# Chunk 0's diagonal score blocks: a copy and a VectorE transpose where a round trip through DRAM stood

## Chip, core and metric

One core of a Trainium2 chip runs the whole kernel. The metric is the device time in microseconds (us) of one execution, lower is better. All arrays are float32. The kernel of before takes 641.42 us, the median of three runs that lie between 640.13 and 642.46 us.

## The reference

A delta-rule attention feeds a two-layer network. Cut to what matters here (B = 4, H = 8, S = 768, D = 48; the network has 384 inputs and 2048 hidden units):

```python
k_n = k / (norm(k, axis=-1) + 1e-06)
state = zeros((B, H, D, D))
for t in range(S):
    y[:, :, t] = einsum('bhd,bhde->bhe', q[:, :, t], state)
    v_old = einsum('bhde,bhd->bhe', state, k_n[:, :, t])
    state = state + beta[:, :, t] * einsum('bhd,bhe->bhde', k_n[:, :, t], v[:, :, t] - v_old)
x = y.transpose(0, 2, 1, 3).reshape(B * S, H * D)
h = x @ w_in
out = (h / (1 + exp(-h))) @ w_out
```

The loop over 768 tokens isn't run token by token. It is cut into six chunks of 128 tokens. Inside a chunk the effect of the tokens on one another is a unit triangular system per head, whose matrix comes from the scores k times k, scaled by a step size beta / |k|^2 (with a minus sign). The inverse of that system is made from 32 x 32 diagonal blocks, and in chunk 0 these again from 16 x 16 ones.

## The kernel before

**Tiles and stages.** A chunk's keys lie in one tile with the tokens on the 128 partitions, the 32 heads (4 batches times 8) along the row. TensorE turns them (`turn`), and multiplies keys with keys (`score` with j = 0) into tiles `ap`, one for two batches (g = 0 or 1); the scores of keys with queries (j = 1) follow. `ap` holds for each head the scores of 64 by 64 tokens, of which the 32 x 32 blocks on the diagonal are wanted first. The four row groups of 32 partitions are numbered j = 0 to 3.

**The way of the diagonal blocks in chunk 0.** `block_out` (lines 569 to 578) writes the blocks from `ap` to a DRAM tile `blocks`, four transfers for each g; in chunk 0 the odd j are issued from ScalarE's queue, the even ones from SyncE's. `block_in` (line 580) reads the DRAM tile back in one transfer of 512 KB into `sums_of_w` at AT_G, now with one head on each partition and its 32 x 32 block along the row. The tile x beside it (AT_X) is cleared by GpSimd and gets ones on its diagonal (lines 564, 565).

**The step sizes.** `square` (GpSimd) and `add_squares` (VectorE) sum the squares of the keys. `norm_steps` (line 395) makes from them, on VectorE, an inverse root by three Newton rounds, the norm n, its reciprocal, and the product with beta. For chunk 0 nothing else stands on VectorE between these. Four instructions at line 423 spread the step sizes by row group, six copies (lines 430, 433) lay n out as `n_slot`; a matmul (`block_steps`, line 442) turns the spread sizes, and ScalarE copies them to `step`.

**The inversion.** `invert_first` (line 663) scales the blocks by the step sizes (line 668), then runs 15 rounds of a product (line 676) and a sum (line 680) on VectorE over two 16 x 16 corners of each block at once, multiplies x by the step sizes (line 683), and transposes x in blocks of 32 x 32, once straight and once turned (lines 690, 694), so that heads and tokens change places again. `joins` then builds the 32 x 32 and 64 x 64 inverses with many small matmuls (`corner`, `turned`, `straight`, `merge_half`), whose results ScalarE and VectorE copy out of PSUM.

**The rest.** `inner`, `update`, `old` and `new` run the chunk's recurrence, `hidden` and `combine` the network; after the prologue TensorE does little else than these. The weights arrive as float32 and are narrowed in pieces by ScalarE, VectorE and GpSimd (`narrow`, lines 233 to 246).

**What sets the order.** Each engine runs its instructions in the order in which the code issues them: `pin` chains them. All loads but a few stand in one line on SyncE's queue (`in_line`); a load given to `paced` also waits for the last TensorE instruction issued before it. Later loads hang on a count of TensorE instructions (`loads`, line 1345). `busy` puts matmuls on TensorE whose results nobody reads. The tile `stage` is free until chunk 1's turned keys are put there.

**Names at the change.** The prologue of chunk 0 is the code from line 1289 to 1380: `first_score` and `block_out`, the loads of the second half of the queries, `add_squares`, `beta_of`, `turn` of the queries, `block_in`, `norm_steps(0)`, `first_queries`, `block_steps(0)`, the clearing of `xis` (line 1332), the loads of w_in, k, and v, and the loop over `invert_first`.

Of the kernel before, what the change touches and what calls it, by code (L numbers as in the profile page):

```python
# [10 lines left out]
FP32 = mybir.dt.float32  # L11
U32 = mybir.dt.uint32
ACTF = mybir.ActivationFunctionType
ALU = mybir.AluOpType
# [5 lines left out]
def kernel(  # L20
# [166 lines left out]
    def load_q(c, bs=ALL):  # L187
        if c < NCH:
            load_pair(queries[c], q, c, bs)
# [197 lines left out]
    def add_squares(c, b):  # L387

        pin(nc.vector.tensor_reduce(
            out=sums[c][:, b * H : (b + 1) * H], in_=squared[c, b], axis=AX.X, op=ALU.add  # L390
        ))

    sizes = {}

    def norm_steps(c):

        seed, t, r = (small.tile([P, BH], kind, name=name, bufs=1)[:] for name, kind in (
            ("seed", U32), ("nt", FP32), ("nr", FP32)
        ))
        ss = sums.pop(c)  # L400
        n = small.tile([P, BH], FP32, name="n", bufs=1)
        by_slot = small.tile([P, 2, B * NP], FP32, name="n_slot", bufs=1)
        yield pin(nc.vector.tensor_scalar(
            out=seed, in0=ss.bitcast(U32), scalar1=-0.5, scalar2=1597463007.0,
            op0=ALU.mult, op1=ALU.add,
        ))
# [12 lines left out]
        yield pin(nc.vector.reciprocal(out=r, in_=n[:]))  # L419
        yield pin(nc.vector.tensor_tensor(out=t, in0=r, in1=beta_tok[:, c, :], op=ALU.mult))  # L420
        for j in range(NB):
            rows = slice(T * j, T * (j + 1))
            yield pin(nc.vector.scalar_tensor_tensor(
                out=spread[rows, place(c, j), :], in0=r[rows], scalar=-1.0, in1=t[rows],
                op0=ALU.mult, op1=ALU.mult,
            ))
        of = n[:].rearrange("p (n e) -> p e n", e=2)
        for g, rows in enumerate(HALVES):
            ns = slice(HB * NP * g, HB * NP * (g + 1))
            yield pin(nc.vector.tensor_copy(out=by_slot[rows, :, ns], in_=of[rows, :, ns]))  # L430
            for hf in range(2):
                rest = HALVES[1 - g]
                yield pin(nc.vector.tensor_copy(out=by_slot[rest, hf, ns], in_=of[rest, 1 - hf, ns]))
        sizes[c] = by_slot

    def place(c, j):
# [117 lines left out]
    def block_room(c):  # L554

        if c == 0:
            g, x = (sum_room[:, at : at + T * T] for at in (AT_G, AT_X))
        else:
            g = work.tile([P, T * T], FP32, name="g", tag="g", bufs=1)[:]
            x = (  # L560
                sum_room[:, AT_LAST : AT_LAST + T * T] if c == 1
                else work.tile([P, T * T], FP32, name="x", tag="x", bufs=1)[:]
            )
        pin(nc.gpsimd.memset(x, 0.0))
        pin(nc.gpsimd.memset(x[:, 0 : T * T : T + 1], 1.0))
        g, x = (t.rearrange("p (s t) -> p s t", t=T) for t in (g, x))
        blocks[c] = (tc.dram_tile([P, T, T], FP32, name=f"blocks{c}"), g, x)

    def block_out(c, g):

        there, ap = blocks[c][0], aps[c, g][0]
        for j in range(NB):
            rows, cols = slice(T * j, T * (j + 1)), slice(T * (j % 2), T * (j % 2 + 1))
            at = T * place(c, j) + HH * g
            issue(
                there[at : at + HH].rearrange("n s t -> s n t"),
                ap[rows].rearrange("s u h t -> s (u h) t")[:, :, cols], c == 0 and j % 2 == 1,
            )

    def block_in(c):  # L580
        there, g, _ = blocks[c]
        in_line(nc.sync.dma_start(out=g, in_=there[:]))
# [80 lines left out]
    def invert_first(step):  # L663
# [2 lines left out]
        g2, x2 = corners(AT_G), corners(AT_X)  # L666
        of = step[:].rearrange("p (i m) -> p i m", i=2)
        yield pin(nc.vector.tensor_tensor(
            out=g2, in0=g2, in1=of.unsqueeze(2).to_broadcast([P, 2, Q, Q]), op=ALU.mult
        ))  # L670
        for m in range(Q - 1, 0, -1):
            n = Q - m
# [10 lines left out]
        yield pin(nc.vector.tensor_tensor(  # L683
            out=x2, in0=x2, in1=of.unsqueeze(3).to_broadcast([P, 2, Q, Q]), op=ALU.mult
        ))
# [603 lines left out]
    def first_score(b):  # L1289

        def evacuate(j, e, to, of):
            (by_dve if e else by_act)(to, of)

        score(0, b, (0,), (A, CC), evacuate)
        if b % HB == 1:
            block_out(0, b // HB)

    busy(3)
    for b in range(B):
        square(0, b)  # L1300
    block_room(0)
    for b in range(2):
        turn(0, b, 0, M, b % 2 == 0)
    first_score(0)
    for b in range(2, B):
        turn(0, b, 0, M, b % 2 == 0)
    for b in range(1, B):
        first_score(b)
        add_squares(0, b - 1)
    load_q(0, slice(HB, B))  # L1310
    add_squares(0, B - 1)
    beta_of(0)

    def first_queries(b):
# [3 lines left out]

        score(0, b, (1,), (A, CC), evacuate)

    for b in range(2):
        turn(0, b, 1, M, b == 0)
    block_in(0)
    busy(1)
    for _ in norm_steps(0):
        pass
    first_queries(0)
    busy(3)
    first_queries(1)
# [12 lines left out]
    for b in range(2, B):  # L1342
# [22 lines left out]
            out=to, in0=to, in1=above[:].unsqueeze(1).to_broadcast([P, H, W]), op=ALU.mult  # L1365
        ))

    for n in range(1 + Q):
        done = next(inv)
        if n in (0, 1, 2, 4, 8):  # L1370
            busy(1, done, Sync)
        if n == 10:
            turn(1, 0, 0, M)
        if n == 12:
            turn(1, 1, 0, M)
        if n == 14:
            turn(1, 2, 0, M)
        if n == 15:
            busy(1, done, Sync)
            turn(1, 3, 0, M)  # L1380
# [258 lines left out]
```

## Time and profile before

| what | value |
|---|---|
| median of the runs | 641.42 us (640.13, 641.42, 642.46) |
| span of the profiled execution, first to last instruction | 636.1 us |
| median less that span | 5.3 us |
| TensorE busy | 622.4 us, 98% |
| VectorE, ScalarE, GpSimd busy | 397.5, 214.3, 89.9 us |
| granted TensorE clock, mean | 0.986 |

The whole time of the profiled execution is not listed beside its span, so the 5.3 us stand for what lies around the span. In the rows that follow a row of the timeline or of the chain of waits begins with the start and the duration in us; a row of the groups gives the total busy time and the mean of one in ns; "x2" is a count of merged instructions. In the windows each engine has its busy us and its number of instructions, then come the granted clock as a share of full speed, the DMA share and GB/s.

### The profile page before, as it was taken

The page shows a single profiled execution, that of the slowest core. Times are in us where ns is not written, and L with a number is a line of the kernel's source. Part 1 is how long each engine was busy: PE and PEld are TensorE (multiplying, and loading weights), DVE is VectorE, ACT ScalarE, POOL GpSimd, SP SyncE. Part 2 cuts the span into 40 slices and gives each one's busy share as a digit, 9 for nine tenths or more (in the row PEclk, how much of TensorE's full clock was granted, in tenths as well). Part 3 has the DMA queues.
Part 4 walks back from the last instruction along what each step waited for, and adds up shares of the span by engine and source line. Part 5 has one row for each costly group of instructions (what it writes and reads, how often), then busy time and mean ns, then how long its engine had stood idle before and what let it go on. Part 6 is the DMA issues. An engine that isn't in the chain of part 4 may idle for free.

```text
span 636.1 us, 21387 instructions
## 1 busy us (share of the span) xinstructions
PE 622.4 (98%) x9406; PEld 547.3 (86%) x9406; DVE 397.5 (62%) x910; ACT 214.3 (34%) x500; POOL 89.9 (14%) x92
## 2 busy tenths in 40 slices
PE   7979999999999999999999999999999999999997
PEld 5568788656799989989989989989989989989997
DVE  5786879999677974546974555975455964112112
ACT  3456673423351122451122451122451122441120
POOL 5033721345020020020020010020002000000000
PEclk9779999999999999999999999999999999999999
DMA  7966726350458460459151359232253133010101
GB/s 114 227 159 177 218 67 148 100 99 4 95 105 174 72 104 8 94 107 183 37 91 21 75 124 164 56 84 29 64 117 76 26 75 37 16 38 1 26 0 26
DMA packets 145676, 54.70 MB, mean 86 GB/s; under 512 B 117152, under 2 KB 138912, under 8 KB 145584
## 3 DMA queue, kind: packets, MB, share of 16 engines
q1 hardware_dynamic: 143136, 52.93, 40.5%
q8 instruction: 74, 1.21, 0.8%
q10 hardware_dynamic: 2448, 0.41, 0.4%
q14 instruction: 18, 0.15, 0.1%
HBM read 40.14 MB, written 11.01 MB: 80 GB/s over the span
## 4 chain that ended last, share of the span: by engine, by line
PE 94%; DVE 2%; DMA 1%; issue 1%; ACTq 0%; ACT 0%; POOL 0%; SPq 0%; DVEq 0%; POOLq 0%
PE phid L1046 40%; PE px L1163 17%; PE py L1163 13%; PE po L1090 5%; PE pb_c L840 3%; PE pa L529 2%; PE pb_c L828 2%; PE pyc L919 2%; PE pb_c L1090 2%; PE pb_c L860 2%; PE pyc L906 1%; PE px L782 1%; PE py L782 1%; PE pt L500 1%; DMA sums_of_w<-blocks 1%
## 5 line engine op out<-in xcount | busy, mean ns | idle before, releaser
L1046 PE MATMUL phid<-xT,w_in 128*128 128x256 f32 x1152 | 257.0, 381 | 0.2 <-DVE xT L893 0.2
L1046 PEld LDWEIGHTS phid<-xT,w_in 128*128 128x128 f32 x1152 | 216.4, 190 | 30.2 <-issue 0.9
L1056 ACT ACTIVATE gT<-phid 128x512 f32<-128x512 f32 x88 | 52.5, 597 | 144.8 <-PE phid L1046 140.5
L1144 DVE TENSOR_TENSOR sums_of_g<-gT 128x384 f32<-128x384 f32 (+1 forms) x60 | 30.4, 529 | 65.7 <-ACT gT L1056 55.4
L627 DVE SCALAR_TENSOR_TENSOR rank<-g,step,x 128x31 f32<-128x31 f32 (+15 forms) x124 | 49.8, 401 | 21.7 <-DMA g<-blocks 18.1
L1163 PE MATMUL px<-sums_of_w,sums_of_g 128*128 128x192 f32 x320 | 56.6, 329 | 0.0
L1163 PE MATMUL py<-w_out,sums_of_g 128*128 128x192 f32 x320 | 56.2, 328 | 0.0
L1163 PEld LDWEIGHTS py<-w_out,sums_of_g 128*128 128x128 f32 x320 | 52.3, 190 | 0.3
L1163 PEld LDWEIGHTS px<-sums_of_w,sums_of_g 128*128 128x128 f32 x320 | 52.2, 190 | 0.4
L632 DVE TENSOR_TENSOR x<-x,rank 128x31 f32<-128x31 f32 (+15 forms) x124 | 42.5, 342 | 4.3
L467 POOL TENSOR_TENSOR vf<-vf,n_slot 128x768 f32<-128x768 f32 x10 | 14.8, 1494 | 174.4 <-DMA vf<-in_v_dram 150.4
L544 ACT COPY xT<-pyc 48x128 f32<-48x128 f32 (+2 forms) x126 | 32.7, 260 | 1.7
L488 DVE STREAM_TRANSPOSE kq<-stage 128x512 f32<-128x512 f32 x28 | 28.4, 1115 | 5.2 <-DMA stage<-in_q_dram 5.2
L1163 PE MATMUL py<-w_out,gT 128*128 128x192 f32 x160 | 28.9, 330 | 0.0
L1174 DVE TENSOR_TENSOR o<-o,kept 128x192 f32<-128x192 f32 (+1 forms) x29 | 11.5, 422 | 26.7 <-ACT kept L1171 26.7
L1163 PE MATMUL px<-w_out,gT 128*128 128x192 f32 x160 | 27.9, 327 | 0.0
L1163 PE MATMUL px<-sums_of_w,gT 128*128 128x192 f32 x160 | 27.8, 327 | 0.0
L1163 PEld LDWEIGHTS px<-w_out,gT 128*128 128x128 f32 x160 | 26.5, 190 | 0.6
L550 POOL COPY g<-x 64x256 f32<-64x256 f32 x4 | 5.0, 1242 | 151.9 <-DVE x L635 151.9
L1163 PEld LDWEIGHTS py<-w_out,gT 128*128 128x128 f32 x160 | 26.1, 190 | 0.4
L865 DVE TENSOR_TENSOR state<-state,pb_c 128x384 f32<-128x384 f32 x22 | 11.2, 550 | 24.1 <-PE pb_c L860 24.1
L1163 PEld LDWEIGHTS px<-sums_of_w,gT 128*128 128x128 f32 x160 | 26.2, 190 | 0.1
(222 smaller groups left out, 931.2 us busy)
## 6 DMA issues: line engine op xcount, KB each, us to landing
vf<-in_v_dram SPq DMA_DIRECT2D x48, 96.0 KB, 2.8
out_dram<-o SPq DMA_DIRECT2D x42, 96.0 KB, 2.2
w_out<-in_moe_w_in_dram SPq DMA_DIRECT2D x4, 768.0 KB, 4.7
sums_of_w<-in_moe_w_out_dram SPq DMA_DIRECT2D x4, 768.0 KB, 4.1
blocks<-ap SPq DMA_DIRECT2D x44, 64.0 KB, 1.9
g<-blocks SPq DMA_DIRECT2D x5, 512.0 KB, 3.5
kb<-in_k_dram SPq DMA_DIRECT2D x12, 192.0 KB, 4.2
kb<-in_k_dram SPq DMA_DIRECT2D x24, 96.0 KB, 4.3
```

Source lines behind the costliest of these rows:

```text
L467: pin(nc.gpsimd.tensor_tensor(out=vf, in0=vf, in1=of, op=ALU.mult))
L488: pin(nc.vector.transpose(out=kqs[c, b][:, :, j, :].rearrange("p a (i m) -> p a m i", i=T), in_=src.rearrange("p a (m d) -> p a m d", d=D) ...
L529: pin(nc.tensor.matmul(pa[e][half, p * n * W : (p + 1) * n * W], lhsT=kq[rows, p, 0, half], rhs=kq[rows, p, js[0] : js[-1] + 1, half], sta ...
L544: return pin(nc.scalar.copy(to, of))
L627: pin(nc.vector.scalar_tensor_tensor(out=tv, in0=g[:, 0:m, m : m + 1].to_broadcast([P, m, n]), scalar=step[:, m : m + 1], in1=x[:, m : m + ...
L632: yield pin(nc.vector.tensor_tensor(out=x[:, 0:m, m:T], in0=x[:, 0:m, m:T], in1=tv, op=ALU.add))
L840: yield pin(nc.tensor.matmul(pz[rows, n * D : (n + 1) * D], lhsT=xis[g][rows, u * H + 2 * p + e, :], rhs=vfs[c][rows, hf, g * HB + u, p, : ...
L1046: pin(nc.tensor.matmul(ph[:, j * GT : (j + 1) * GT], lhsT=w_in[:, a, (2 * f + j) * P : (2 * f + j + 1) * P], rhs=xTs[c, hf][:, a, :], star ...
L1056: pin(nc.scalar.activation(out=hidden_of(c, hf, f), in_=ph[:], func=ACTF.Silu, scale=-0.5 if in_blocks(c) else 0.5))
L1090: pin(nc.tensor.matmul(pos[i][:, 0:DM], lhsT=hidden_of(0, hf, f // 2)[:, at : at + C], rhs=w_outs[f // HFF][:, f % HFF, :], start=(f == 0) ...
L1144: pin(nc.vector.tensor_tensor(out=sums_of_g[:, k, fs], in0=of[0], in1=of[1], op=op))
L1163: pin(nc.tensor.matmul(to, lhsT=at, rhs=quarter(f, *b) if isinstance(b, tuple) else sums_of_w[b][:, f], start=start and f == 0, stop=f == ...
```

## The change

Chunk 0 no longer sends its diagonal blocks through DRAM. A view `diagonal` of the tile `stage` takes them: eight copies of 32 partitions by 512 elements, from `ap` (32 of each 64 columns) to a dense row, six on GpSimd (all four of g = 0, the first two of g = 1) and two on ScalarE. One VectorE transpose in 32 x 32 blocks then puts heads on the partitions and writes the place from which `invert_first` reads. The step sizes of chunk 0 are made by one VectorE instruction on all partitions and turned by one VectorE transpose into `step`; the four spreading instructions, the matmul and ScalarE's copy are gone for chunk 0, and the six copies to `n_slot` go to GpSimd.

GpSimd writes the step sizes on x's diagonal instead of ones, so that the last multiplication of x by them falls away. In exchange, the blocks are scaled along their other index (`unsqueeze(3)` for `unsqueeze(2)` at line 668).

The order moves too. The second half of the queries is loaded at the start of the prologue; the loads of w_in 0, keys 1, w_in 1 and v 0 are issued ahead of the queries' turning, w_in 0 without `paced`. The four `add_squares` stand between the turns and scores. ScalarE takes both of the first two turns of queries out of PSUM. One `busy` matmul is added before the last two turns.

```diff
-        for j in range(NB):
+        if c == 0:
+            size = small.tile([P, T], FP32, name="step")
+            pin(nc.vector.scalar_tensor_tensor(
+                out=t, in0=r, scalar=-1.0, in1=t, op0=ALU.mult, op1=ALU.mult
+            ))
+            pin(nc.vector.transpose(out=size[:], in_=t))
+            step_of[0] = size
+        for j in range(NB if c > 0 else 0):
...
+        engine = nc.vector if c > 0 else nc.gpsimd
...
-            yield pin(nc.vector.tensor_copy(out=by_slot[rows, :, ns], in_=of[rows, :, ns]))
+            yield pin(engine.tensor_copy(out=by_slot[rows, :, ns], in_=of[rows, :, ns]))
...
-        pin(nc.gpsimd.memset(x[:, 0 : T * T : T + 1], 1.0))
+        if c > 0:
+            pin(nc.gpsimd.memset(x[:, 0 : T * T : T + 1], 1.0))
...
-            out=g2, in0=g2, in1=of.unsqueeze(2).to_broadcast([P, 2, Q, Q]), op=ALU.mult
+            out=g2, in0=g2, in1=of.unsqueeze(3).to_broadcast([P, 2, Q, Q]), op=ALU.mult
...
-        yield pin(nc.vector.tensor_tensor(
-            out=x2, in0=x2, in1=of.unsqueeze(3).to_broadcast([P, 2, Q, Q]), op=ALU.mult
-        ))
...
-        if b % HB == 1:
-            block_out(0, b // HB)
+    diagonal = stage[:, 0 : BH * T].rearrange("p (n t) -> p n t", t=T)
+
+    def diagonal_blocks(g, engines):
+
+        for j, by in enumerate(engines):
+            rows, cols = slice(T * j, T * (j + 1)), slice(T * (j % 2), T * (j % 2 + 1))
+            by(diagonal[rows, HH * g : HH * (g + 1)], aps[0, g][0][rows].rearrange("s u h t -> s (u h) t")[:, :, cols])
+
+    load_q(0, slice(HB, B))
     busy(3)
     for b in range(B):
         square(0, b)
     block_room(0)
+    add_squares(0, 0)
     for b in range(2):
         turn(0, b, 0, M, b % 2 == 0)
+    add_squares(0, 1)
     first_score(0)
     for b in range(2, B):
         turn(0, b, 0, M, b % 2 == 0)
-    for b in range(1, B):
-        first_score(b)
-        add_squares(0, b - 1)
-    load_q(0, slice(HB, B))
+    add_squares(0, 2)
+    first_score(1)
+    diagonal_blocks(0, (by_pool, by_pool, by_pool, by_pool))
+    first_score(2)
+    first_score(3)
+    diagonal_blocks(1, (by_pool, by_pool, by_act, by_act))
     add_squares(0, B - 1)
     beta_of(0)
...
+    fetch_w_in(0)
+    load_k(1)
+    fetch_w_in(1)
+    load_v(0)
     for b in range(2):
-        turn(0, b, 1, M, b == 0)
-    block_in(0)
+        turn(0, b, 1, M)
...
-    step = block_steps(0)
+    step = step_of[0]
+    of_step = blocks[0][2].rearrange("p s t -> p (s t)")[:, 0 : T * T : T + 1]
+    pin(nc.gpsimd.tensor_copy(out=of_step, in_=step[:]))
+    pin(nc.vector.transpose(
+        out=blocks[0][1].rearrange("p s t -> p t s"), in_=diagonal.rearrange("p n t -> p t n")
+    ))
     for t in xis:
         pin(nc.gpsimd.memset(t, 0.0))
-    paced(fetch_w_in, 0)
-    load_k(1)
-    fetch_w_in(1)
-    load_v(0)
     for c in range(1, NCH):
         beta_of(c)
-    busy(1)
+    busy(2)
...
-    for n in range(1 + Q):
+    for n in range(Q):
```

More of the change, by code (lines that the diff above doesn't have):

```diff
@@ L391, in add_squares @@
         ))
-    sizes = {}
+    sizes, step_of = {}, {}
     def norm_steps(c):
@@ L429, in norm_steps @@
             ns = slice(HB * NP * g, HB * NP * (g + 1))
-            yield pin(nc.vector.tensor_copy(out=by_slot[rows, :, ns], in_=of[rows, :, ns]))
+            yield pin(engine.tensor_copy(out=by_slot[rows, :, ns], in_=of[rows, :, ns]))
             for hf in range(2):
                 rest = HALVES[1 - g]
-                yield pin(nc.vector.tensor_copy(out=by_slot[rest, hf, ns], in_=of[rest, 1 - hf, ns]))
+                yield pin(engine.tensor_copy(out=by_slot[rest, hf, ns], in_=of[rest, 1 - hf, ns]))
         sizes[c] = by_slot
@@ L564, in block_room @@
         pin(nc.gpsimd.memset(x, 0.0))
[L565 removed]
+        if c > 0:
+            pin(nc.gpsimd.memset(x[:, 0 : T * T : T + 1], 1.0))
         g, x = (t.rearrange("p (s t) -> p s t", t=T) for t in (g, x))
[L567 removed]
+        blocks[c] = (tc.dram_tile([P, T, T], FP32, name=f"blocks{c}") if c > 0 else None, g, x)
     def block_out(c, g):
@@ L576, in block_out @@
                 there[at : at + HH].rearrange("n s t -> s n t"),
-                ap[rows].rearrange("s u h t -> s (u h) t")[:, :, cols], c == 0 and j % 2 == 1,
+                ap[rows].rearrange("s u h t -> s (u h) t")[:, :, cols],
             )
```

## The prediction

> **What bounds the kernel now.** I read the page first, for the share of each engine over the whole and the chain that ended last.
>
> ```profile
> span 636.1 us, 21387 instructions
> PE 622.4 (98%) x9406; PEld 547.3 (86%) x9406; DVE 397.5 (62%) x910; ACT 214.3 (34%) x500; POOL 89.9 (14%) x92
> PE 94%; DVE 2%; DMA 1%; issue 1%; ACTq 0%; ACT 0%; POOL 0%; SPq 0%; DVEq 0%; POOLq 0%
> ```
>
> TensorE is the bound, and the change takes no work from it but one matmul. So it can only pay where the chain leaves TensorE: the 2% of VectorE and 1% of DMA. The chain of waits of the first 95 us shows where that is.
>
> ```profile
> 10.68 0.44 DVE ap L547
> 11.18 0.38 ACTq L104
> 14.14 2.76 DMA blocks<-ap
> 17.05 4.91 DMA sums_of_w<-blocks
> 22.06 0.70 DVE sums_of_w L668
> 22.85 0.22 DVE rank L676
> 31.52 0.99 DVE sums_of_w L683
> 32.54 1.04 DVE sums_of_w L690
> 33.58 1.82 DVE sums_of_w L694
> 52.46 1.53 PE phid L1046 x6
> ```
>
> The last row is the first matmul of the hidden layer. From 11.18 us on, the end hangs on the eight transfers out, then on the one back, which lands at 21.96; only then can VectorE scale the blocks (22.06) and begin the rounds (22.85). It ends the last transpose at 35.40. What moves these two ends moves all behind them, as long as nothing else becomes late: from there the chain goes through TensorE to the end, and the later loads hang on TensorE's count, so they move along. So I ask when the rounds begin, and how long they take. For that I read the timeline of VectorE from 10 to 23 us.
>
> ```profile
> 12.27 0.41 DVE L547 COPY ap<-pb_c 128x256 f32<-128x256 f32 x1
> 12.60 1.00 DVE L389 TENSOR_REDUCE ss<-sq 128x8 f32<-128x384 f32 x2
> 13.52 0.68 DVE L506 TENSOR_SCALAR kq<-pt 128x512 f32<-128x512 f32 x1
> 14.11 0.17 DVE L403 TENSOR_SCALAR seed<-ss 128x32 uint32<-128x32 uint32 x1
> 16.80 0.35 DVE L419 RECIPROCAL nr<-n 128x32 f32<-128x32 f32 x1
> 17.26 0.19 DVE L420 TENSOR_TENSOR nt<-nr,beta_tok 128x32 f32<-128x32 f32 x1
> 17.49 0.77 DVE L423 SCALAR_TENSOR_TENSOR spread<-nr,nt 32x32 f32<-32x32 f32 x4
> 22.06 0.69 DVE L668 TENSOR_TENSOR sums_of_w<-sums_of_w,step 128x512 f32<-128x512 f32 x1 [3.01 <-DMA sums_of_w<-blocks]
> ```
>
> The norm takes 14.11 to 17.49: fourteen instructions, 12 of them up to the reciprocal in 2.69 us, 0.224 each. VectorE is free at 19.05 and waits 3.01 us. So the transfers hide the norm now; without them the norm itself is late next.
>
> **The change part by part.** *The way through DRAM* goes: 8 transfers out, one in, and ScalarE's two stops for issuing them. *The end of the scores.* Two of the four reductions (0.5 each by the row with x2) go ahead into gaps in which VectorE waited for TensorE, and the query copy of 0.68 goes to ScalarE. So the copy that starts at 12.27 can start as soon as the last scores are there, and TensorE's row for them is the first here; the second is a ScalarE copy of the size of the new ones:
>
> ```profile
> 11.30 0.22 PE L529 MATMUL pb_c<-kq 48*64 48x64 f32 x1
> 141.88 0.62 ACT L544 COPY xi<-up 32x512 f32<-32x512 f32 x1
> ```
>
> They end at 11.52; the copy ends at 11.95, the last reduction at 12.45, and the norm begins near 12.5 in place of 14.11. ScalarE, freed of issuing, makes its two copies (0.62 each) after its last score copy near 11.95 and reaches beta near 13.2, before VectorE asks for it.
>
> *If nothing disturbed it,* the norm's 3.38 us end at 15.9; the product on all partitions and the small transpose are two more steps of 0.23 (a 128x32 instruction), 16.35; the transpose of the blocks has the shape of line 694, 1.82 on the chain, 18.2; the scaling 0.79 (22.06 to 22.85), 19.0. The rounds begin 3.85 early. At the end the multiplication by the step sizes is gone: 31.52 to 32.54, 1.02. Together 4.87. That is the bound on the good side.
>
> *But six copies now stand on GpSimd beside the norm.* What one costs I take from the groups, and how GpSimd and VectorE get on with each other from their timelines at 128 us, where GpSimd has instructions back to back and VectorE rounds of the same kind as here.
>
> ```profile
> L550 POOL COPY xi<-up 32x512 f32<-32x512 f32 x2 | 1.6, 777 | 8.4 <-DVE up L607 8.4
> L691 POOL COPY sums_of_w<-pick 128x512 f32<-128x512 f32 x1 | 0.6, 632 | 18.3 <-DVE rank L676 18.3
> L550 POOL COPY g<-x 64x256 f32<-64x256 f32 x4 | 5.0, 1242 | 151.9 <-DVE x L635 151.9
> L334 POOL COPY pick<-ident 32x32 f32<-32x32 f32 x4 | 0.8, 203 | 0.2
> 127.98 1.88 POOL L246 TENSOR_TENSOR w_out<-w_out,sums_of_w 128x768 int32<-128x768 int32 x1 [1.62 <-ACT sums_of_w L234]
> 129.82 3.09 POOL L467 TENSOR_TENSOR vf<-vf,n_slot 128x768 f32<-128x768 f32 x2
> 276.33 2.91 POOL L467 TENSOR_TENSOR vf<-vf,n_slot 128x768 f32<-128x768 f32 x2 [45.43 <-DMA vf<-in_v_dram]
> 128.20 1.86 DVE L632 TENSOR_TENSOR sums_of_w<-sums_of_w,rank 128x175 f32<-128x175 f32 x1
> 130.09 1.48 DVE L627 SCALAR_TENSOR_TENSOR rank<-g,step,sums_of_w 128x156 f32<-128x156 f32 x1
> 131.61 1.48 DVE L632 TENSOR_TENSOR sums_of_w<-sums_of_w,rank 128x156 f32<-128x156 f32 x1
> 133.12 0.36 DVE L627 SCALAR_TENSOR_TENSOR rank<-g,step,sums_of_w 128x135 f32<-128x135 f32 x1
> ```
>
> Three VectorE instructions that would need under 0.4 us (the row at 133.12 is such a one) end at 130.06, 131.57 and 133.09: each 0.2 or so after a GpSimd instruction ended (129.86, then about 131.2 and 132.91). One VectorE instruction gets through per GpSimd instruction, while GpSimd loses only 0.09 each (3.09 against 2.91 for the pair). The Trainium skill, "SBUF — State Buffer", section "Who interferes with whom", says that a VectorE instruction with two SBUF inputs and a GpSimd one that reads SBUF block each other for the whole instruction; it speaks against this change, and by it the sum is the smaller one below, without it the 4.87. The trace agrees, by the three rows.
>
> Twelve of the norm's instructions, with the new product, have two inputs in SBUF. The copies can begin at 11.15, when the second batch's scores are out (10.68 + 0.44 on the chain) and GpSimd is free of clearing x, as its row shows.
>
> ```profile
> 10.08 0.95 POOL L564 MEMSET sums_of_w<- 128x1024 f32 x1
> ```
>
> A copy has the shape of the 777 ns row, of which some is the same quarrel, since VectorE copied beside it; 632 ns is the bound below, 1242 ns (a column read across the row) the one above. I take a pace of 0.76 per copy, hold-up included, nearest the row of its own shape. Six end at 15.7. In that time the norm passes its seed and one further instruction at the end of each copy from the third to the sixth: four, the last ending at 15.9. Seven remain to n, 7 x 0.224, 17.45; the reciprocal 0.46 (16.80 to 17.26), 17.9. Now the six copies to `n_slot`, which waited for n on GpSimd, run beside it at about 0.2 each (the 203 ns row): the two products wait some 0.12 each, 18.6; the small transpose 18.85; the blocks 20.7; the scaling 21.5. The rounds begin 22.85 - 21.5 = 1.35 early, and with the 1.02 the sum is 2.37, call it 2.4. Bounds by the pace: 0.70 gives 2.7, 1.31 (the 1242 ns row with the hold-up) gives a loss, worked out below.
>
> *Costed at nothing:* the small copy that writes x's diagonal (0.2) and the clearing of `xis` are queued on GpSimd behind `n_slot` and end under the transpose of the blocks (1.82); without that cover the 0.2 would count. Who waits for the diagonal is the first round at 21.5. The scaling along the other index has the same operands and count. The 16 transfers of w_in 0, keys 1, w_in 1 and v 0 that are pulled ahead on SyncE's queue stand in front of nothing that the prologue reads; the second half of the queries comes earlier, and TensorE no longer waits for it as here:
>
> ```profile
> 20.84 0.63 PE L500 MATMUL pt<-ident,z 128*128 128x128 f32 x4 [0.41 <-DMA z<-in_q_dram]
> ```
>
> That wait lies off the chain, so it earns nothing. The extra `busy` matmul is hidden in TensorE's own wait for the first round.
>
> So the span becomes 636.1 - 2.4 = 633.7. The median of the runs stands 5.3 above the span of before; with that unchanged the time is 639.0 us.
>
> **The rivals.** *A: the lock doesn't bite.* If the small products of 0.19 us slip between copies, or the copies are done by the time that they come, the whole 4.87 is had: 636.5 us. For it: the first two copies are over before the norm begins. Against: the rows at 128 us, and no row with two inputs that ran free beside such a GpSimd instruction.
>
> *B: the copies are slow and the norm waits longer than the transfers did.* Place: GpSimd's six copies. At 1.31 each they end at 19.0; the norm has five of its two-input steps by then (19.2), n comes at 20.55, the reciprocal at 21.0, the products 21.7, the turned step size 21.95, the blocks 23.8, the scaling 24.6: 1.75 late, less 1.02, a loss of 0.7, 642.1 us. Between a pace of 0.76 (gain 2.4) and 1.31 (loss 0.7) the point from which the time is lost lies near 1.18. For it: the only other strided copy on GpSimd took 1242 ns. Against: that one reads single columns, while these read runs of 32 elements, as the 777 ns row writes them.
>
> *C: the clock eats it.* TensorE's granted clock falls twice in the start.
>
> ```profile
> 21.00:22.00 1.00, 1.00 (x8) 0.88 (x7) 0.00 (x0) 0.50 (x1) 0.00 (x0) 0.69 0.95 336
> 28.00:29.00 1.00, 1.00 (x4) 0.61 (x3) 0.90 (x4) 0.00 (x0) 0.00 (x0) 0.90 0.91 218
> 38.00:39.00 1.00, 0.09 (x11) 0.00 (x0) 0.97 (x2) 0.73 (x2) 0.37 (x1) 0.72 0.73 215
> 48.00:49.00 1.00, 1.00 (x50) 1.00 (x52) 0.87 (x2) 0.00 (x0) 0.00 (x0) 0.66 0.06 16
> ```
>
> Between 21.4 and 28.2, and between 38.4 and 48.7, it is half: 6.8 and 10.3 us, two and three steps of 3.4. The first fall lies under VectorE's rounds; the second lies on the small matmuls of the chain. Where work moves against these steps, one step more at half clock costs up to 1.7 us, one less gains as much: 640.7 or 637.3. The Trainium skill, "TensorE: Matmul & The Clock Gate", section "What's actually happening", has a free-running window of 3413 ns that decides by the activity in it; the trace agrees with its 6.8 and 10.3 us. Against a loss: TensorE's work moves as a whole, so the step is as likely to help. A loss of one step is what I count as C, 640.7.
>
> **How the numbers follow.** Chances: the forecast 0.50, A 0.20, B 0.13, C 0.17. About 0.3%, 1.9 us, is what a measurement of this kernel can tell from no change; so faster means under 639.5, slower over 643.3. The forecast's own range is 638.2 to 640.0 (paces of 0.70 to 0.90), and I put 0.38 of its 0.50 under 639.5; with A that is 0.58. Slower takes 0.08: the part of B where the clock also loses a step (642.1 + 1.7 = 643.8) and 0.03 for what I have not seen. The rest, 0.34, is within 0.3%. The range reaches from a little below A, 636.0, to B, 642.2.
>
> **What would show it.** In the changed profile I expect: no transfer of blocks before 70 us; six copies of GpSimd from 11.15 to about 15.7 at 0.65 to 0.8 each; instructions of the norm at 0.6 to 0.8 us beside them and 0.19 after; the transpose of the blocks at 18.85, the scaling at 20.7, the first round at 21.5; the rounds themselves unchanged, 8.7 us; the last transpose ending near 33.0 and the same lead kept at the first hidden-layer matmul (52.46 before). Wrong would be: a norm with 0.19 throughout (A); copies over 1.18 us (B); rounds that begin early while the lead is lost between 33 and 52 us (C, or a wait that I have not named). Wrong altogether would be a transpose of the blocks that isn't what VectorE waits for, but ScalarE's two copies or beta.

## The result, and the profile after

| | before | changed |
|---|---|---|
| median of the runs, us | 641.13 (20 runs, 639.34 to 642.46) | 638.86 (20 runs, 636.76 to 640.35) |
| ratio, 95% interval | | 0.9965 (0.9955 to 0.9975) |
| profiled execution: its time, span | not listed, 636.1 | 638.56, 636.8 |

The changed kernel is 2.27 us faster; 639.0 was forecast. Two spans of profiled executions can't show that: 636.1 before stands against 636.8 after. Every later run gives its time beside its span: the difference is 1.8 us here (638.56 - 636.8), 1.7 to 1.9 in all kernels but that of experiment 6, which has 2.1 to 2.2. The 5.3 us that the prediction put "around the span" were therefore mostly something else: the first trace of before shows an execution of about 637.9 us (an estimate, 636.1 + 1.8), quicker than any of the 20 runs in the table. So the kernel before was traced a second time, and the changed kernel too.

> The kernel before, for a second trace. Theory (the first trace of before was a quick execution: its span of 636.1 us lies 3 us under what its median leaves): the head is as in the first trace (first round 22.8, last transpose ends 35.4 us, both within 0.3), and the 3 us show behind it, on the way to the first hidden-layer matmul or after 94 us, where single waits come and go. Rival (before's own head is slower as a rule than its first trace showed): the first round begins after 23.3 us.

> The changed kernel unchanged, beside the next three, for a second trace and a second set of times on the same chip. Theory: the gain over before is 2.3 us, give or take 0.6; the first round begins at 20.8 us, the last transpose ends near 32.3, and TensorE's clock is half for three or four steps of 3.4 us between 33 and 50 us. Rival (the trace of after was an odd one): the first round or the last transpose move by more than 0.3 us.

Run again, the kernel before took 640.86 us against itself at 640.59 (ratio 0.9996, 0.9982 to 1.0011); the changed kernel 637.93 against 640.63 (0.9955, 0.9944 to 0.9967). Their spans, 639.1 and 636.8, now lie as the medians do. In both traces the start differs from the first trace by more than the 0.3 us that the expectations allowed: before begins its rounds at 22.38 where it had 22.85, the changed kernel at 21.29 where it had 20.78. For the changed kernel that is the rival on record. Of its 0.51 us, 0.35 lie ahead of the norm (the first keys land later and the squares start at 6.65, 6.24 in the first trace); the norm itself has the other 0.16.

First the page of the changed kernel: the span, the engines' busy times, the chain's shares by engine.

```profile
span 636.8 us, 21379 instructions
PE 620.8 (97%) x9406; PEld 545.9 (86%) x9406; DVE 398.3 (63%) x901; ACT 216.1 (34%) x502; POOL 94.7 (15%) x104
PE 94%; DVE 3%; issue 1%; DMA 1%; ACT 0%; SPq 0%; POOL 0%; POOLq 0%; DVEq 0%
```

TensorE's 94% is as before; VectorE's share of the chain has grown from 2% to 3%: the norm stands on it now, where the transfers of the blocks stood. The timeline of VectorE in the changed kernel shows that norm and what follows it.

```profile
12.07 0.54 DVE L389 TENSOR_REDUCE ss<-sq 128x8 f32<-128x384 f32 x1
12.65 0.18 DVE L403 TENSOR_SCALAR seed<-ss 128x32 uint32<-128x32 uint32 x1
12.87 0.48 DVE L409 SCALAR_TENSOR_TENSOR nt<-ss,seed 128x32 f32<-128x32 f32 x1
13.39 0.62 DVE L412 TENSOR_TENSOR nt<-nt,seed 128x32 f32<-128x32 f32 x1
14.04 0.62 DVE L413 SCALAR_TENSOR_TENSOR nr<-nt,seed 128x32 f32<-128x32 f32 x1
14.69 0.61 DVE L409 SCALAR_TENSOR_TENSOR nt<-ss,nr 128x32 f32<-128x32 f32 x1
15.34 0.19 DVE L412 TENSOR_TENSOR nt<-nt,nr 128x32 f32<-128x32 f32 x1
...
16.70 0.18 DVE L418 TENSOR_SCALAR n<-nt 128x32 f32<-128x32 f32 x1
...
18.00 1.94 DVE L1353 STREAM_TRANSPOSE sums_of_w<-stage 128x1024 f32<-128x1024 f32 x1
19.98 0.69 DVE L677 TENSOR_TENSOR sums_of_w<-sums_of_w,step 128x512 f32<-128x512 f32 x1
20.78 0.21 DVE L685 TENSOR_TENSOR rank<-sums_of_w 128x30 f32<-128x30 f32 x1
...
30.36 1.95 DVE L700 STREAM_TRANSPOSE sums_of_w<-sums_of_w 128x1024 f32<-128x1024 f32 x1
```

The GpSimd timeline of the changed kernel has the six copies beside it, and ScalarE's has its two.

```profile
11.36 3.90 POOL L558 COPY stage<-ap 32x512 f32<-32x512 f32 x6
...
18.21 0.24 POOL L1352 COPY sums_of_w<-step 128x32 f32<-128x32 f32 x1
```

```profile
12.25 1.24 ACT L552 COPY stage<-ap 32x512 f32<-32x512 f32 x2 [0.19 <-DVE ap L555]
13.52 0.20 ACT L364 ACTIVATE beta_tok<-pb 128x32 f32<-128x32 f32 x1
```

The six copies end at 15.26, 0.65 each. Between 12.87 and 15.30 four instructions of the norm get through, at 0.48 to 0.62 us; those after it take 0.19. The reduction above them has one input and takes 0.54, as without the copies (experiment 3). The seed, with one input too, begins here as the second copy ends (12.66) and takes 0.18. In the second trace of the changed kernel it begins just after that (12.99) and is held up like the others. This is VectorE there, and the copies beside it:

```profile
13.00 0.64 DVE L403 TENSOR_SCALAR seed<-ss 128x32 uint32<-128x32 uint32 x1
13.68 0.62 DVE L409 SCALAR_TENSOR_TENSOR nt<-ss,seed 128x32 f32<-128x32 f32 x1
...
14.98 0.61 DVE L413 SCALAR_TENSOR_TENSOR nr<-nt,seed 128x32 f32<-128x32 f32 x1
```

```profile
11.71 3.84 POOL L558 COPY stage<-ap 32x512 f32<-32x512 f32 x6 [0.75 <-DVE ap L555]
```

Four get through beside the last four copies here as well, but the seed is one of them. It takes 0.64 in experiment 4 too. So two inputs are not the whole condition; experiment 8 comes back to this.

Blocks (15.26) and beta (13.72) are there long before VectorE asks for them, so the norm alone sets when the rounds begin: 20.78. What was 35.40 in the first trace of before, the end of the last transpose, is now 32.31. The chain of waits of the second trace of before shows the same places, with the last row from near 95 us, where the long runs of hidden-layer matmuls begin.

```profile
16.45 5.05 DMA sums_of_w<-blocks
...
22.38 0.21 DVE rank L676
33.10 1.81 DVE sums_of_w L694
53.05 1.53 PE phid L1046 x6
95.58 4.51 PE phid L1046 x20
```

And the chain of the changed kernel at the two later places.

```profile
50.68 1.53 PE phid L1052 x6
93.05 7.10 PE phid L1052 x32
```

The lead over this trace is 22.38 - 20.78 = 1.6 us at the first round, 34.91 - 32.31 = 2.6 at the last transpose, 53.05 - 50.68 = 2.4 at the first hidden matmul, 95.58 - 93.05 = 2.5 near 95 us, and 639.1 - 636.8 = 2.3 at the end. What is won in the first 33 us reaches the end nearly whole. Against the first trace it shrank from 3.1 to 1.8 by the first hidden matmul and was gone at the end; that was that execution's doing. The two traces of before part in the same way: the second is 0.5 us ahead at the last transpose, 0.6 behind at the first hidden matmul, 1.4 behind near 95 us and 3.0 at the end.

The traces of all kernels at these places (us; "way" is the time from the last transpose to the second half of xT, the input of the hidden layer):

| | first round | last transpose ends | way | xT written | span |
|---|---|---|---|---|---|
| before, first trace | 22.85 | 35.40 | 16.9 | 52.32 | 636.1 |
| before again | 22.38 | 34.91 | 18.0 | 52.90 | 639.1 |
| changed | 20.78 | 32.31 | 18.2 | 50.54 | 636.8 |
| changed again | 21.29 | 32.80 | 17.9 | 50.66 | 636.8 |
| final product back | 20.79 | 33.33 | 18.5 | 51.85 | 637.1 |
| product gone alone | 22.39 | 33.89 | 17.6 | 51.48 | 637.2 |
| no GpSimd copies | 19.22 | 30.75 | 18.3 | 49.00 | 633.8 |
| loads late | 20.54 | 32.06 | 18.6 | 50.64 | 638.4 |
| four copies by ScalarE | 20.16 | 31.70 | 17.8 | 49.48 | 635.1 |
| the same, x cleared earlier | 19.55 | 31.07 | 19.4 | 50.47 | 637.9 |
| roots in PSUM | 18.95 | 30.47 | 19.9 | 50.33 | 636.1 |

### The profile page after: what moved, and what is told of

It reads as the page before. It is cut to its first block, busy times and chain, and to the rows that moved or that the text cites. A ratio compares the mean times of both kernels' runs of the same rounds, so it can differ in the third digit from the quotient of the medians.

```text
span 636.8 us, 21379 instructions
## 1 busy us (share of the span) xinstructions
PE 620.8 (97%) x9406; PEld 545.9 (86%) x9406; DVE 398.3 (63%) x901; ACT 216.1 (34%) x502; POOL 94.7 (15%) x104
## 4 chain that ended last, share of the span: by engine, by line
PE 94%; DVE 3%; issue 1%; DMA 1%; ACT 0%; SPq 0%; POOL 0%; POOLq 0%; DVEq 0%
PE phid L1052 40%; PE px L1169 17%; PE py L1169 13%; PE po L1096 5%; PE pb_c L846 3%; PE pa L537 3%; PE pb_c L834 2%; PE pyc L925 2%; PE pb_c L1096 2%; PE pb_c L866 2%; PE pyc L912 1%; PE px L788 1%; PE py L788 1%; PE pb_c L537 1%; PE pt L508 1%
```

## The experiments

**1. The final product back.** The step sizes leave x's diagonal; the multiplication after the rounds stands again.

```diff
-        if c > 0:
-            pin(nc.gpsimd.memset(x[:, 0 : T * T : T + 1], 1.0))
+        pin(nc.gpsimd.memset(x[:, 0 : T * T : T + 1], 1.0))
...
-            out=g2, in0=g2, in1=of.unsqueeze(3).to_broadcast([P, 2, Q, Q]), op=ALU.mult
+            out=g2, in0=g2, in1=of.unsqueeze(2).to_broadcast([P, 2, Q, Q]), op=ALU.mult
...
+        yield pin(nc.vector.tensor_tensor(
+            out=x2, in0=x2, in1=of.unsqueeze(3).to_broadcast([P, 2, Q, Q]), op=ALU.mult
+        ))
...
-    of_step = blocks[0][2].rearrange("p s t -> p (s t)")[:, 0 : T * T : T + 1]
-    pin(nc.gpsimd.tensor_copy(out=of_step, in_=step[:]))
...
```

> The changed kernel with one part undone: ones on x's diagonal, the blocks scaled along the old index, and the last multiplication of x by the step sizes back. Theory (the lead at VectorE's last transpose is 2.07 us from rounds that begin early and 1.02 us from the product that is gone; what is left of it reaches the end one for one): the last transpose ends 1.0 us later than in the changed kernel (near 33.3 us in place of 32.3) and the gain over before falls from 2.3 to about 1.2 us. Rival (the clock's steps decide, a microsecond of lead is not worth a microsecond): the gain stays within 0.4 us of 2.3, or goes altogether.

637.93 us against 639.85 (0.9975, 0.9960 to 0.9989). The chain of waits of this kernel, behind the last sum of the rounds:

```profile
29.45 0.99 DVE sums_of_w L691
30.47 1.04 DVE sums_of_w L698
```

The product costs 30.47 - 29.45 = 1.02 on VectorE, and xT comes 1.2 to 1.3 later than in the changed kernel. In the time the theory isn't borne out: the gain over before is 1.9 us, within the 0.4 of 2.3 that the rival allowed, and not about 1.2. Experiment 4, the changed kernel but for its loads and measured beside the same runs of before, gains 2.25; against that the product costs 0.3 us, and the intervals overlap.

**2. That part alone, on the kernel before.** The step sizes go on x's diagonal, the blocks are scaled along the other index, the product is gone; nothing else of the change.

```diff
-        pin(nc.gpsimd.memset(x[:, 0 : T * T : T + 1], 1.0))
+        if c > 0:
+            pin(nc.gpsimd.memset(x[:, 0 : T * T : T + 1], 1.0))
...
-        yield pin(nc.vector.tensor_tensor(
-            out=x2, in0=x2, in1=of.unsqueeze(3).to_broadcast([P, 2, Q, Q]), op=ALU.mult
-        ))
...
+    of_step = blocks[0][2].rearrange("p s t -> p (s t)")[:, 0 : T * T : T + 1]
+    pin(nc.gpsimd.tensor_copy(out=of_step, in_=step[:]))
```

> The kernel before with one part of the change alone: GpSimd puts the step sizes on x's diagonal, the blocks are scaled along the other index, and the last product is gone; the way through DRAM stays. Theory: the first round stays at 22.85 us (the step sizes are there by 19.0 and the diagonal by 19.3, the transfer lands at 21.96), the last transpose ends 1.02 us earlier (34.4), and the time falls by 1.0 us, give or take 0.6. Rival (the scaling along the other index costs what the product saved, or the diagonal comes late): no change.

640.67 us against 640.59 (0.9995, 0.9982 to 1.0008). The last transpose ends at 33.89, 1.02 before the 34.91 of "before again", and xT comes 1.4 earlier; in the time 1.0 us was expected and none is seen (the interval reaches from 1.2 us faster to 0.5 slower). The 1.02 us are shown at VectorE, twice; that the end gets them is not.

**3. GpSimd's copies taken away.** The copies of ScalarE stay; six of the eight blocks' rows are zeros, written early. This asks what the copies cost the norm.

```diff
-    diagonal_blocks(0, (by_pool, by_pool, by_pool, by_pool))
...
-    diagonal_blocks(1, (by_pool, by_pool, by_act, by_act))
+    diagonal_blocks(1, (None, None, by_act, by_act))
```

> The changed kernel without GpSimd's six copies into the dense tile: that part of it is cleared early instead, so chunk 0's inverse is made from a quarter of the blocks only. Theory of the lock: the four norm steps that took 0.48, 0.62, 0.62 and 0.61 us take 0.19 each, the norm and all behind it come 1.5 us earlier than in the changed kernel (first round near 19.2 us instead of 20.78), and the gain over before is 3.3 to 3.9 us. Rival (they waited for something else, such as ScalarE or the reductions): the four steps stay above 0.4 us and the first round stays near 20.8.

635.92 us against 639.85 (0.9941, 0.9926 to 0.9956). VectorE's timeline of this kernel:

```profile
12.91 0.19 DVE L410 SCALAR_TENSOR_TENSOR nt<-ss,seed 128x32 f32<-128x32 f32 x1
...
13.82 0.19 DVE L413 TENSOR_TENSOR nt<-nt,nr 128x32 f32<-128x32 f32 x1
...
19.22 0.20 DVE L686 TENSOR_TENSOR rank<-sums_of_w 128x30 f32<-128x30 f32 x1
```

The same four instructions go from 12.91 to 13.82, 0.91 us, in place of 12.87 to 15.34, 2.47: the hold-up is 1.56, and the first round comes 1.56 earlier than in the changed kernel. All of it reaches xT (49.00 against 50.54). In the time it is 3.9 us below before, where the changed kernel's two measurements have 2.3 and 2.7.

**4. The loads late.** w_in 0 paced again, and the loads of w_in 0, keys 1, w_in 1 and v 0 back where they were.

```diff
-    fetch_w_in(0)
-    load_k(1)
-    fetch_w_in(1)
-    load_v(0)
     for b in range(2):
...
         pin(nc.gpsimd.memset(t, 0.0))
+    paced(fetch_w_in, 0)
+    load_k(1)
+    fetch_w_in(1)
+    load_v(0)
```

> The changed kernel with the loads of w_in 0, keys 1, w_in 1 and v 0 put back to their old place, w_in 0 again waiting for TensorE. Theory (these loads stand in front of nothing that the path reads): no change against the changed kernel, a gain over before of 2.3 us, give or take 0.5. Rival (part of the gain is that weights and v lie ready earlier): the gain falls under 1.5 us and waits for w_in or vf show between 32 and 60 us.

637.60 us against 639.85 (0.9973, 0.9958 to 0.9988), and first round, last transpose and xT stand as in the changed kernel. The early loads are not where the gain is. Its trace has a span of 638.4 for another reason; the chain of waits shows it.

```profile
91.58 3.52 DMA xT<-part
95.24 5.81 PE phid L1052 x18
```

TensorE stood still from 93.54 to 95.24 for one transfer of xT; the window from 96 to 97 us then has a granted clock of 0.50. The changed kernel's two traces have no such wait there.

**5. Fewer copies on GpSimd.** ScalarE makes all four of the second half.

```diff
-    diagonal_blocks(1, (by_pool, by_pool, by_act, by_act))
+    diagonal_blocks(1, (by_act, by_act, by_act, by_act))
```

> The changed kernel with all four copies of the second half on ScalarE, so that GpSimd makes four. Theory of the lock: only two norm steps are held up instead of four, the first round begins 0.85 us earlier (near 19.9 us) and the gain over before grows to about 3 us, unless ScalarE's copies, now four of 0.62 us from 12.2 on, bring beta later than VectorE asks for it (near 16.5 us). Rival (the transposes wait for the copies, not the norm): the first round does not move, or moves later.

638.65 us against 639.85 (0.9976, 0.9959 to 0.9993): a gain of 1.2 us where about 3 was expected, so not faster than the changed kernel. VectorE's timeline shows the lock where it was foreseen, with two norm steps held up and not four.

```profile
13.08 0.48 DVE L409 SCALAR_TENSOR_TENSOR nt<-ss,seed 128x32 f32<-128x32 f32 x1
13.60 0.62 DVE L412 TENSOR_TENSOR nt<-nt,seed 128x32 f32<-128x32 f32 x1
14.25 0.19 DVE L413 SCALAR_TENSOR_TENSOR nr<-nt,seed 128x32 f32<-128x32 f32 x1
```

The rounds begin at 20.16, 0.62 earlier (0.85 was expected). In this execution the lead also reached xT, written at 49.48, 1.1 earlier than in the changed kernel; 0.6 of it stands at VectorE's first instruction behind the transposes (L730, 31.57 against 32.18), the rest came with a clock that was half for 10.2 us and not 13.7. Why the median shows none of it, this trace doesn't tell; the next experiment has a trace in which the lead is lost.

**6. The same, and x cleared before the squares,** while GpSimd waits for keys, so that its copies can start sooner.

```diff
     busy(3)
+    block_room(0)
     for b in range(B):
         square(0, b)
-    block_room(0)
```

> The changed kernel with four GpSimd copies in place of six (ScalarE makes all of the second half) and x cleared before the squares, while GpSimd waits for the keys, so that the copies begin 0.2 us earlier. Theory of the lock: one or two norm steps are held up, the first round begins at 19.9 us or earlier, 0.9 before the changed kernel, and the gain over before is about 3 us. Rival (what is won at the head is lost behind it, as in the run with four copies): first round as said, and a gain of no more than 2.3 us.

639.22 us against 640.59 (0.9971, 0.9956 to 0.9987). The rounds begin at 19.55 and the last transpose ends at 31.07, 1.2 earlier than in the changed kernel, yet xT is written at 50.47, against 50.54 and 50.66 there. That is the rival: the gain is 1.4 us and not about 3. The chain of waits of this kernel no longer passes through the norm.

```profile
13.78 0.61 ACT stage L552
14.41 0.20 ACT beta_tok L364
14.61 0.50 ACT kq L518
15.85 3.41 PE pb_c L347 x6
31.48 0.13 PE pl L723 x2
32.16 0.08 DVE sums_of_w L730
```

ScalarE's four copies (the last at 13.78) make the query copies behind them late, TensorE's scores wait for those, and TensorE then comes to the corner matmuls (L723) only at 31.41; VectorE waits 1.09 us for them, and its first instruction behind the transposes starts at 32.16, as in the changed kernel (32.18).

The late query copies are not all of it. The six rows of `busy` at 15.85 take 3.41 us here and 2.20 in the changed kernel (at 14.88), and the window on them shows why.

```profile
17.00:18.00 1.00, 1.00 (x3) 0.56 (x2) 1.00 (x1) 0.00 (x0) 1.00 (x2) 0.50 1.08 170
```

The granted clock is half from 16.5 to 20.0. From these `busy` matmuls to the next of beta (L361) TensorE needs 4.36 us (15.78 to 20.14), and 2.76 both in the changed kernel and in experiment 5: the 1.60 between them are more than the 1.09 that VectorE waited. In experiment 5 TensorE waits as long for the query copies, at full clock, and the lead stands. So in this trace the half clock, and not the late query copies alone, takes the lead away. TensorE had stood 2.0 us for the query copies just before, and a third trace with four copies on ScalarE (the second kernel of experiment 7) shows such a fall (17.3 to 20.7) after the same wait, while no trace with six copies on GpSimd has one there. That the wait brings the fall, and that this is what the medians of both experiments show, was not tested.

How much room TensorE had is told by the view of what TensorE waits for between 10 and 51 us, first in the changed kernel, then in this one.

```profile
PE pb_c L347 <- DVE sums_of_w L689: 1.3, 1, 1.3
PE pa L537 <- ACT kq L518: 1.0, 2, 0.8
```

```profile
PE pa L537 <- ACT kq L518: 2.3, 2, 2.0
```

A row gives the total wait, the number of waits and the longest. In the changed kernel TensorE stands 1.3 us at a `busy` matmul that is paced by the rounds: so much later it may come without cost. Here, and in experiment 5, the wait for the query copies has grown by 1.3 and the other row is gone. In experiment 3 that row is gone too, with nothing in its place, and there VectorE's 1.56 us reached xT whole.

**7. Fuller TensorE, against the clock.** The granted clock is half for 13.7 us between 34 and 48 us in the changed kernel. Nine more matmuls whose results nobody reads were spread over that stretch, in the changed kernel, in that of experiment 5, and in the kernel before.

```diff
...
+        if n == 13:
+            busy(1, done, Sync)
...
-        lambda: (),
+        lambda: busy(2, room=M),
...
-        lambda: (fill(1),),
+        lambda: (fill(1), busy(3, room=M),),
...
-        lambda: (fill(1), begin_next(),),
+        lambda: (fill(1), begin_next(), busy(3, room=M),),
```

> The changed kernel with nine more matmuls whose result nobody reads, put where TensorE waits between the last rounds and the merges (one at round 13, two after the corners, three after the straight products, three after the first merges). Theory (the half clock over the merges costs part of the lead): the half clock between 34 and 48 us is shortened or gone, the way from the last transpose to the first hidden-layer matmul falls from 18.4 us to under 17.4, and the time falls by 1 to 2 us against the changed kernel. Rival (the merges wait for VectorE and ScalarE, not for TensorE's clock): the clock rises, the way stays within 0.4 us of 18.4 and the time doesn't change; or the added matmuls get in the way and it grows.

> The same nine matmuls, and ScalarE makes all four copies of the second half as in the run of that change alone, whose first round began 0.6 us early without a gain that could be measured. Theory (the 0.6 us are there, and were lost in the clock's steps): 0.6 us faster than the kernel with the nine matmuls alone. Rival (ScalarE's later copies cost elsewhere): no faster, or slower, with a later evacuation of the first query scores to show for it.

> The kernel before with the same nine matmuls in the same places. With the clock dealt with alike on both sides the difference to the changed kernel with nine matmuls is the lead of the change alone. Theory: 3.1 us between the two (2.07 from the rounds, 1.02 from the product). Rival (the lead is really 2.3 and the clock is no part of it): 2.3 us or less between the two, and this kernel gains nothing over before.

648.45, 646.93 and 649.53 us against 640.63 (ratios 1.0121, 1.0107, 1.0131): all slower by 6 to 9 us. The windows from 33 to 47 us, of the changed kernel and of the first of the three (TensorE's busy time first, the granted clock behind GpSimd's):

```profile
33.00:47.00 14.00, 11.24 (x428) 10.79 (x430) 11.12 (x22) 6.25 (x15) 4.11 (x3) 0.54 0.54 146
```

```profile
33.00:47.00 14.00, 11.71 (x383) 8.46 (x381) 9.06 (x18) 6.33 (x14) 4.23 (x3) 1.00 0.57 143
```

The clock came up from 0.54 to 1.00, and still the way to xT grew to 19.6 us, for the added matmuls stand in the chain of waits themselves, three of them (six rows of the trace) for 2.13 us at 37.63 and three more at 41.48. Most of the loss comes later: the first hidden matmul starts 1.7 us later than in the changed kernel, the span is 10.9 longer. The added matmuls also count in TensorE's count on which the later loads hang, so this experiment is no clean test of the clock. Where the rest goes was not followed. The difference for which the third kernel was made, before against changed with nine matmuls each, is 1.1 us on four runs each, where 3.1 was expected; with a loss of this size it tells nothing about the lead.

**8. The lock taken away, the copies left in place.** The seed and the root of the norm lie in PSUM, so no norm instruction has two inputs in SBUF.

```diff
             ("seed", U32), ("nt", FP32), ("nr", FP32)
         ))
+        if c == 0:
+            spare = kept_banks["c0"]
+            seed, r = (spare[:, DM + BH * i : DM + BH * (i + 1)] for i in range(2))
+            seed = seed.bitcast(U32)
```

> The changed kernel with nothing left out; in chunk 0 the seed and the root (seed, nr) of the norm lie in PSUM, in 64 columns of a bank that no matmul writes, so that no instruction of the norm has more than one input in SBUF. The six GpSimd copies stay where they are. Theory (VectorE waits for GpSimd only where it reads two inputs from SBUF): no instruction of the norm is held up though the copies run beside it, each takes about 0.2 us, the four that took 0.48 to 0.62 too; the first round comes 1.3 to 1.6 us earlier than in the changed kernel, near 19.2 to 19.6 us, the last transpose ends near 30.9; ratio to the kernel before 0.993 to 0.995. Rival 1 (any VectorE instruction is held up beside these copies, or inputs in PSUM are dearer by as much): four instructions of 0.5 us or more again, first round near 20.8, ratio 0.9955 to 0.9965. Rival 2 (the lead is gained at VectorE and lost at TensorE, as where ScalarE made four copies): first round near 19.4, but the way from the last transpose to xT longer by a microsecond, ratio 0.996 or above.

638.98 us against 640.75 (0.9977, 0.9963 to 0.9990). VectorE's timeline of this kernel, and the GpSimd row beside it:

```profile
12.66 0.19 DVE L413 SCALAR_TENSOR_TENSOR nt<-ss,pb_c 128x32 f32<-128x32 f32 x1
12.88 0.19 DVE L416 TENSOR_TENSOR nt<-nt,pb_c 128x32 f32<-128x32 f32 x1
13.11 0.20 DVE L417 SCALAR_TENSOR_TENSOR pb_c<-nt,pb_c 128x32 f32<-128x32 f32 x1
13.34 0.19 DVE L413 SCALAR_TENSOR_TENSOR nt<-ss,pb_c 128x32 f32<-128x32 f32 x1
...
18.95 0.20 DVE L689 TENSOR_TENSOR rank<-sums_of_w 128x30 f32<-128x30 f32 x1
```

```profile
11.14 3.84 POOL L562 COPY stage<-ap 32x512 f32<-32x512 f32 x6
```

All six copies run from 11.14 to 14.98, and the four instructions beside them take 0.19 and 0.20. The seed, which begins at 12.43, just as the second copy ends, writes to PSUM here and takes 0.20. So VectorE as such is not held up: an instruction is that reads two inputs from SBUF, or, as the seed in the second trace, one input from SBUF and writes there. The Trainium skill, "SBUF — State Buffer", section "Who interferes with whom", draws the line much the same way: two SBUF inputs contend with a GpSimd instruction that reads SBUF, at most one does not outside VectorE's 2-port modes, and `tensor_scalar` is among the operations that can enter these. The rows agree for two inputs and for the seed's 0.64; that the seed ran in such a mode no row shows.

The rounds begin at 18.95, 1.83 earlier than in the changed kernel (1.58 of it in the norm, from the seed's start to n's end 2.65 us in place of 4.23), and the time is no better than that kernel's. TensorE's timeline shows a part of the reason: the bank with the roots is, against the expectation, one that `busy` writes, in other columns.

```profile
16.06 2.20 PE L347 MATMUL pb_c<-state,ident 128*128 128x384 f32 x6 [1.32 <-DVE nt L427]
```

In the changed kernel this group starts at 14.88. The edit made TensorE wait 1.32 us for the norm's last reader and spent TensorE's room of 1.3; VectorE then waits 0.36 for TensorE behind the transposes, and the way to xT became 19.9. The second rival on record, a lead gained at VectorE and lost behind it, is what happened. How it is lost is only in part traced: of the 1.83, 1.34 stand at the first instruction behind the transposes (30.84 against 32.18), 0.85 at the first half of xT (47.30 against 48.15) and 0.21 at the second. The same with a bank that no matmul of the prologue touches was not tried, so whether a kernel that makes all its copies can have the 1.56 us stays open.

## Why the prediction was right

*What bounds it, and what is late next.* Right: the transfers are gone from the prologue (the first transfer of blocks now starts at 73.38 us), and the norm is what VectorE waits for, not ScalarE's copies, beta, or the blocks.

*The lock.* Right in the count: "at the end of each copy from the third to the sixth: four" was forecast, four are held up in each trace, the last ending at 15.30 (15.9 forecast). Which four is right for the first trace; in the second the seed, which the prediction let pass, is the first of them. Experiments 3 and 8 show the cause from two sides. Rival A (no hold-up, 636.5 us) falls with that; experiment 3 is what it looks like, 3.9 us below before.

*The pace of a copy.* This term was mis-sized: 0.65 and not 0.76, nearer the contiguous 632 ns copy than the strided 777 ns row. With n forecast at 17.45 and there at 16.88, the rounds begin 0.7 (second trace 0.2) before the 21.5 forecast. Rival B, from 1.18 per copy on, was far off.

*The product that is gone.* 1.02 at VectorE, as forecast. In the time it is not shown (experiments 1 and 2).

*The sum.* 1.35 + 1.02 = 2.37 was forecast. Mean over the two traces of each kernel: the rounds begin (22.62 - 21.04) = 1.6 early and the last transpose ends (35.16 - 32.56) = 2.6 early; the medians differ by 2.27 and 2.70. So the term of the rounds was 1.35 and is 1.6. That the time is hit to 0.1 us is in part luck: the sum was 0.2 short at the last transpose, and the 641.42 us it started from, of three runs, are 641.13 over twenty.

*The median less the span.* The step "the median of the runs stands 5.3 above the span of before; with that unchanged" was wrong in what it took the 5.3 for: 1.8 lie around the span, and some 3.5 were the distance of one quick execution from the median. It cancels, because 636.1 + 5.3 is the median again, and 641.4 - 2.4 is 639.0. Had the changed kernel's time been checked against its own span plus 5.3, it would have come out 642.1.

*The clock, rival C.* The forecast's half-clock times came from that same trace. Behind the transposes the clock is half for 10.2 us in the first trace of before, for 13.7 in the second and in the changed kernel's two. The step that the changed kernel seemed to lose, "before again" lost too, so the change does not cost it. The first fall that the prediction read, 21.4 to 28.2 us, is in none of these other three.

*Costed at nothing.* The diagonal copy (18.21 to 18.45) lies under the transpose of the blocks, as said; the early loads neither help nor harm (experiment 4). "The extra `busy` matmul is hidden in TensorE's own wait" held, and that wait, 1.3 us, is the room that experiments 5, 6 and 8 spent.

## What to carry to other kernels

When a round trip through memory is replaced by engine work, cost the next wait, here a chain of small VectorE instructions, and count those that will stand beside GpSimd work: with two SBUF inputs, and the seed here with one, each got through only as one GpSimd copy ended. A lead on one engine can be lost on the engine that it hands over to, by a wait or by a half clock; read that engine's waits and its granted clock before spending effort on more. And hold a span only against the time of its own execution: a second trace of the kernel before settled what two spans had turned round.

## What was not expected of the hardware

Executions of one kernel differ by 3 to 5 us (638.93 to 644.18 over 29 of before), with the granted clock's mean between 0.983 and 0.989 and single waits as that of 1.70 us in experiment 4; differences under a microsecond, as the product's, stayed out of reach with 12 runs. And TensorE can be busy 11.24 of 14 us with small matmuls at a granted clock of 0.54, while 11.71 busy us that hold wide ones had 1.00.
